# An RWKV recurrence and a SwiGLU layer on one core: single-token w, x transposed by DMA, and a new order of the steps

## The chip, the cores and the metric

The kernel runs on one core of one Trainium2 chip. A core has five engines that take their instructions in order, each from its own queue: TensorE (PE, matrix products, with its weight loads shown as PEld), VectorE (DVE), ScalarE (ACT), GpSimd (POOL) and SyncE (SP), which here only starts DMAs. They wait for one another by semaphores. The metric is the device time of one execution in microseconds (us). Three executions of the kernel before took 205.27, 206.77 and 207.02 us; their median is 206.77 us.

## The reference

Four batches, eight heads, 768 tokens, head dimension 48. Each head carries a 48 x 48 state through the tokens; the output of all heads of a token is a row of 384 numbers, which goes through RMS normalisation and a SwiGLU layer with 1536 hidden units.

```python
for t in range(S):
    cur = einsum('bhd,bhe->bhde', u * k[t], v[t])
    y[t] = einsum('bhd,bhde->bhe', r[t], state + cur)
    state = w[t][..., None] * state + einsum('bhd,bhe->bhde', k[t], v[t])
x = y, heads side by side          # 3072 tokens x 384
xn = x / sqrt(mean(x * x) + 1e-6) * rms_g
out = (silu(xn @ w_gate) * (xn @ w_val)) @ w_out
```

## The kernel before

The 768 tokens are cut into six superblocks of 128. A step such as `q_mm.2.1` is the function `q_mm` for superblock n = 2 and batch j = 1; one (n, j) is called a chunk. The kernel has no loops over chunks: a long string `ORDER` (lines 25 to 128) lists every step, and the kernel calls them one after another, so each engine's queue has its instructions in the order of that string. The PSUM banks are given out by rings (`psum`, line 223) to steps as they come, and tile pools give out SBUF buffers; a step that takes a buffer waits until its last reader is done.

**Recurrence of one chunk.** `load_w`, `load_r`, `load_k`, `load_v` (lines 252 to 271) start DMAs on SyncE's queue. `ln` (383) takes the logarithm of w on ScalarE. `cs_mm` (391) sums the logarithms over tokens with TensorE, `exp_r` and `exp_k` (426, 433) take exponentials on ScalarE, and `r_mul`, `k_mul` (444, 449) multiply r and k by them, with `k_mul` on VectorE or GpSimd by the table `K_POOL`. r and k are then transposed: for superblocks 0 and 1 by TensorE (`rk_pe`, 470), with a copy out of PSUM by `rk_tr` (476), for the others by a DMA transpose in `rk_tr`. `q_mm` (485) multiplies r with k for all pairs of tokens, `q_mask_e`, `q_copy_o` and `q_mask_o` (498 to 511) cut it to earlier tokens, `st_mm` and `st_new` (513, 523) carry the state, `y_mm` (532) forms y, and `bonus_mul`, `bonus_sum`, `bonus_v` (455 to 468, mostly GpSimd) form the term with u, which `x_add` (543) adds.

**w in pairs of tokens.** For superblocks 0 and 1 (`WIN = (0, 1)`, line 181) one load of 384 KB per batch brings w of both, with two consecutive tokens in a partition, one `ln` serves both, and `cs_mm` needs two matmuls for each sum and a second sum for k. For superblocks 2 to 5 each chunk has its own load of 192 KB and its own `ln`; `cs_mm` makes one sum, and `cs_add` (420) gets the sum for k from it on VectorE:

```python
if n in WIN:
    t = inp["w", 0, j] = pin.tile([128, 2 * DM], FP32, name="wt", bufs=NIN // 2)
    o = t.rearrange("p (h x) -> p h x", h=H)
    src = w[j, :, 0:2 * L, :].rearrange("h (p i) d -> p h (i d)", i=2)
```

**Normalisation.** `x_sq`, `x_rstd` and `xn_mul` (548 to 563) scale a chunk's x. For superblocks 0 to 3, `xn_pe` (574) transposes it on TensorE into PSUM, three matmuls, and `xn_out` (580) takes it out on VectorE, multiplied by rms_g. For superblocks 4 and 5, `xn_tr` (571) transposes it by a DMA on SyncE's queue, and `xn_gain` (591) multiplies it by rms_g in place, on GpSimd. Which of the two a chunk takes is only a matter of the steps that stand in `ORDER`.

**The layer.** Four chunks (512 tokens) make a group; there are six. For each group, `gate_mm` and `val_mm` (605, 609; the matmuls are at line 602) make twelve products each of three matmuls, `silu` (613) runs on ScalarE, `h_mul` (617) on VectorE; then `o_mm` (630) makes four output products of twelve matmuls, `o_out` copies them out and `out_dma` stores them. Groups 0 and 1 are made of batches 0, 1 and of batches 2, 3 of superblocks 0 and 1 (`COL`, line 193), so that group 0 can start before batches 2 and 3 have been loaded. While the products of one group run, the recurrence of the next superblock is worked between them. The weights come by `load_gv` and `load_wo` (348, 356) on GpSimd's DMA queue. ScalarE has two function tables, one for logarithm and exponential and one for silu, and `act` (232) loads a table whenever the other is in place. Steps called `warm` are matmuls of zeros that compute nothing.

The lines of the engines' steps are those of the profile, except that activations show the line of `act` (236).

## Time and profile before

| | |
|---|---|
| median of three executions | 206.77 us |
| the profiled execution | 206.26 us |
| its span, first to last instruction | 204.5 us |
| TensorE busy | 191.3 us, 94% |
| VectorE busy | 151.7 us, 74% |
| ScalarE busy | 144.4 us, 71% |
| GpSimd busy | 126.6 us, 62% |
| first gate matmul | 30.89 us after the start of the span |
| last group's first gate matmul | 178.00 us |

Times inside the span are counted from its start. The profile covers one execution. A busy TensorE need not be at its peak, since matmuls are pipelined and a matmul's duration is longer than the distance to the next one; what a step costs TensorE is read from start to start. A row of the timeline has start, length, engine, line, operation, output and inputs, shapes and count, and in square brackets how long the engine was idle before it and what ended that. A row of groups has the count, the busy time, the mean length of one in ns, and the idle time before. "DMA to landing" counts from issue until the data is there.

### The profile page before, as it was taken

What the parts mean: (1) busy time and instruction counts of PE and PEld (TensorE: products, weight loads), DVE (VectorE), ACT (ScalarE), POOL (GpSimd) and SP (SyncE); (2) the same over time, 40 slices, a digit from 0 to 9 for tenths busy, and PEclk for the clock granted to TensorE, in tenths of its full rate; (3) what the DMA queues carried; (4) which work ended last, traced back from release to release, by engine and by line L of the source; (5) the groups of instructions that cost most, each with busy time, mean ns of one, the idle gap of its engine ahead of it and who ended that gap; (6) DMA issues with size and microseconds to landing.
All of it is one profiled execution on the core that took longest, in us unless ns stands there. A gap on an engine that the chain in (4) does not pass through costs nothing.

```text
span 204.5 us, 4369 instructions
## 1 busy us (share of the span) xinstructions
PE 191.3 (94%) x1553; PEld 113.5 (55%) x1573; DVE 151.7 (74%) x298; ACT 144.4 (71%) x287; POOL 126.6 (62%) x186
## 2 busy tenths in 40 slices
PE   1995989999999999999999989999999999899996
PEld 1563654566665565664565644655655556455564
DVE  5169886599897999988999799978886782045720
ACT  4278797699998599977667697997885664046401
POOL 6569696279669954898892693769997736300000
PEclk9998599999999999999999999999999999999999
DMA  6999999999997999999979997985396310201212
GB/s 148 239 222 229 196 179 205 191 194 194 188 187 170 185 186 197 214 192 212 208 160 219 227 208 160 213 189 114 69 196 125 90 23 20 77 0 74 83 58 98
DMA packets 121566, 32.41 MB, mean 158 GB/s; under 512 B 116420, under 2 KB 120392, under 8 KB 121544
## 3 DMA queue, kind: packets, MB, share of 16 engines
q1 hardware_dynamic: 119504, 28.58, 66.8%
q0 software_dynamic: 2032, 3.54, 9.8%
q8 instruction: 12, 0.20, 0.4%
q14 instruction: 10, 0.08, 0.1%
q10 hardware_dynamic: 8, 0.00, 0.0%
HBM read 25.96 MB, written 4.72 MB: 150 GB/s over the span
## 4 chain that ended last, share of the span: by engine, by line
PE 69%; DMA 12%; POOL 8%; DVE 3%; issue 3%; ACT 2%; POOLq 1%; SPq 0%; DVEq 0%; ACTq 0%
PE ps_bu L602 10%; PE ps_av L602 9%; PE ps_au L602 9%; PE ps_bv L602 9%; PE ps_qz L634 5%; DMA wv_sb<-in_moe_w_val_dram 5%; PE ps_qx L634 4%; PE ps_qu L634 3%; DMA wo_sb<-in_moe_w_out_dram 3%; PE ps_qv L634 3%; DMA vt<-in_v_dram 2%; POOL ruk L458 2%; DMA rkT<-rk 1%; POOL ruk L457 1%; DMA xnt<-xn 1%
## 5 line engine op out<-in xcount | busy, mean ns | idle before, releaser
L620 DVE TENSOR_TENSOR ht<-ps_bu,sg 128x512 bf16<-128x512 f32 x38 | 26.1, 686 | 16.9 <-PE ps_bu L602 12.8
L634 PEld LDWEIGHTS <-ht 128*128 128x128 bf16 x300 | 28.3, 98 | 17.2 <-issue 0.4
L602 PEld LDWEIGHTS <-wg_sb 128*128 128x128 bf16 x216 | 23.7, 114 | 22.7 <-issue 2.3
L236 ACT ACTIVATE sg<-ps_av 128x512 bf16<-128x512 f32 x38 | 22.7, 597 | 14.0 <-PE ps_av L602 11.9
L602 PEld LDWEIGHTS <-wv_sb 128*128 128x128 bf16 x216 | 22.4, 115 | 17.9 <-DMA wv_sb<-in_moe_w_val_dram 0.4
L602 PE MATMUL ps_av<-xnt,wg_sb 128*128 128x512 bf16 x111 | 30.5, 379 | 0.4 <-DVE xnt L588 0.2
L602 PE MATMUL ps_bu<-xnt,wv_sb 128*128 128x512 bf16 x103 | 30.2, 381 | 0.6
L457 POOL TENSOR_TENSOR ruk<-rt,kt 128x384 f32<-128x384 f32 x24 | 24.7, 1028 | 9.2 <-DMA rt<-in_r_dram 8.7
L620 DVE TENSOR_TENSOR ht<-ps_bv,sg 128x512 bf16<-128x512 f32 x34 | 23.3, 686 | 8.5 <-PE ps_bv L602 5.2
L602 PE MATMUL ps_au<-xnt,wg_sb 128*128 128x512 bf16 x97 | 27.0, 380 | 1.2 <-POOL xnt L593 0.8
L236 ACT ACTIVATE sg<-ps_au 128x512 bf16<-128x512 f32 x34 | 20.3, 597 | 10.4 <-PE ps_au L602 8.3
L602 PE MATMUL ps_bv<-xnt,wv_sb 128*128 128x512 bf16 x101 | 27.6, 381 | 0.0
L458 POOL TENSOR_TENSOR ruk<-ruk,u_bc 128x384 f32<-128x384 f32 x24 | 24.6, 1024 | 1.9
L467 POOL TENSOR_TENSOR ydiag<-vt,diag 128x384 f32<-128x384 f32 x24 | 19.8, 831 | 5.7 <-DVE diag L462 5.7
L234 ACT ACT_TABLE_LOAD x16 | 20.5, 1283 | 1.9 <-PEq L673 1.6
L510 POOL TENSOR_SCALAR_AFFINE_SELECT qts<-qts 128x512 bf16<-128x512 bf16 x20 | 12.6, 638 | 13.3 <-ACT qts L503 13.3
L634 PE MATMUL ps_qz<-wo_sb,ht 128*128 128x384 bf16 x96 | 17.1, 326 | 0.2 <-DMA wo_sb<-in_moe_w_out_dram 0.2
L563 ACT ACTIVATE xn<-xb,rstd 128x384 bf16<-128x384 f32 x24 | 14.3, 606 | 3.8 <-POOL rstd L559 3.6
L550 ACT ACTIVATE junk<-xb 128x384 bf16<-128x384 f32 x24 | 12.4, 518 | 6.0 <-DVE xb L545 5.5
L634 PE MATMUL ps_qx<-wo_sb,ht 128*128 128x384 bf16 (+1 forms) x84 | 13.8, 315 | 0.0
L462 DVE TENSOR_REDUCE diag<-ruk 128x8 f32<-128x384 f32 x24 | 12.8, 542 | 0.5 <-POOL ruk L458 0.5
L236 ACT ACTIVATE lw<-wt 128x384 bf16<-128x384 f32 (+1 forms) x20 | 11.4, 579 | 1.5 <-DMA wt<-in_w_dram 1.4
(155 smaller groups left out, 370.4 us busy)
## 6 DMA issues: line engine op xcount, KB each, us to landing
kt<-in_k_dram SPq DMA_DIRECT2D x24, 192.0 KB, 4.2
rt<-in_r_dram SPq DMA_DIRECT2D x24, 192.0 KB, 3.9
vt<-in_v_dram SPq DMA_DIRECT2D x24, 192.0 KB, 3.8
out_dram<-ob SPq DMA_DIRECT2D x23, 192.0 KB, 3.0
wt<-in_w_dram SPq DMA_DIRECT2D x16, 192.0 KB, 4.1
wt<-in_w_dram SPq DMA_DIRECT2D x4, 384.0 KB, 4.2
wo_sb<-in_moe_w_out_dram POOLq DMA_DIRECT2D x3, 384.0 KB, 6.8
wg_sb<-in_moe_w_gate_dram POOLq DMA_DIRECT2D x1, 768.0 KB, 10.4
```

Source lines behind the costliest of these rows:

```text
L234: nc.scalar.preload_act_table_set(table_name)
L236: return nc.scalar.activation(**kw).ins
L457: nc.gpsimd.tensor_tensor(out=ruk[n, j], in0=inp["r", n, j], in1=inp["k", n, j], op=ALU.mult)
L458: nc.gpsimd.tensor_tensor(out=ruk[n, j], in0=ruk[n, j], in1=u_bc, op=ALU.mult)
L462: nc.vector.tensor_reduce(out=diag[n, j].rearrange("p h o -> p (h o)"), in_=ruk[n, j], axis=mybir.AxisListType.X, op=ALU.add)
L467: nc.gpsimd.tensor_tensor(out=ydiag[n, j], in0=inp["v", n, j], in1=diag[n, j].to_broadcast([128, H, D]), op=ALU.mult)
L510: nc.gpsimd.affine_select(out=qts[n, j][:, 1], in_=qts[n, j][:, 1], compare_op=ALU.is_gt, fill=0.0, base=0, pattern=[[0, NP], [1, 128]], c ...
L550: nc.scalar.activation(out=junk, in_=xb[n, j], func=AF.Square, accum_out=rstd[n, j][:, 0:1])
L563: nc.scalar.activation(out=xn, in_=xb[n, j], func=AF.Copy, scale=rstd[n, j][:, 1:2])
L602: nc.tensor.matmul(ps, lhsT=units(ws, c, f), rhs=xnt[n].rearrange("p (c x) -> p c x", c=KC)[:, c, :], start=(c == 0), stop=(c == KC - 1))
L620: nc.vector.tensor_tensor(out=ht[n][:, f, :], in0=bank.pop(("v", n, f)), in1=bank.pop(("sg", n, f)), op=ALU.mult)
L634: nc.tensor.matmul(ps[:, cols], lhsT=ht[n][:, f, b * L:(b + 1) * L], rhs=wo_sb[:, f, cols], start=(f == 0), stop=(f == FC - 1))
```

## The change

1. **w of batches 2 and 3 by single tokens.** `WIN` and `ONE_SUM` become sets of chunks. Superblocks 0 and 1 of batches 2 and 3 are loaded, logged and summed like those of the later superblocks: four loads of 192 KB in place of two of 384 KB, four `ln` of 384 columns in place of two of 768, one sum instead of two in each of the four `cs_mm`, and four more `cs_add`.
2. **x of superblocks 2 and 3 transposed by DMA.** Eight `xn_pe` and eight `xn_out` give way to eight `xn_tr` and eight `xn_gain`. `xn_gain` runs on VectorE for the chunks in `GAIN_DVE` (eight chunks of superblocks 2 to 5) and on GpSimd for the other eight.
3. **Other engines for single steps.** Four copies of transposed r and k go from ScalarE to VectorE (`RK_DVE`), three k products from VectorE to GpSimd (`K_POOL`), casts of v from seven on ScalarE to nine, the normalisation's square root from six on ScalarE to three, and output copies from thirteen on VectorE to eleven.
4. **A new order of all steps.** The first matmuls with u and rms_g become steps (`u_mm`, `u_out`, `g_mm`, `g_out`) that stand in the order too. More input loads stand ahead of the first gate matmul (37 instead of 24 loads), the `warm` steps that stood at the end of the order stand further ahead, and the function tables change 14 times instead of 16. Unused options are taken out, and `HALF`, which is empty, is put in.

```diff
-    CAST_ACT = sel("00 10 20 21 40 41 42")
+    CAST_ACT = sel("03 10 11 12 40 42 43 52 53")
-    K_POOL = sel("02 03 20 21 23 31 33 41 51 52 53")
+    K_POOL = sel("02 12 13 20 21 30 31 33 41 42 43 50 52 53")
-    WIN = (0, 1)
+    WIN = sel("00 01 10 11")
-    ONE_SUM = (2, 3, 4, 5)
+    ONE_SUM = sel("02 03 12 13 20 21 22 23 30 31 32 33 40 41 42 43 50 51 52 53")
-    GAIN_POOL = (4, 5)
+    GAIN_DVE = sel("21 22 23 33 41 42 50 51")
-    RK_DVE = sel("")
+    RK_DVE = sel("01 02 03 12")
-    RSTD_ACT = sel("00 01 02 11 32 42")
-    OUT_DVE = sel("00 01 02 10 11 13 21 22 33 40 43 50 53")
+    RSTD_ACT = sel("00 01 10")
+    OUT_DVE = sel("10 12 13 23 30 32 42 50 51 52 53")
+    HALF = ()
...
-        if n in WIN:
+        if (n, j) in WIN:
...
-        if n not in ONE_SUM:
+        if (n, j) not in ONE_SUM:
...
-    u_ps = psum("q", None, [128, DM])
-    nc.tensor.matmul(u_ps, lhsT=ones_row, rhs=u_row, start=True, stop=True)
-    nc.vector.tensor_copy(out=u_bc.rearrange("p h d -> p (h d)"), in_=u_ps)
...
+    def u_mm(n, j):
+        ps = bank["u", n, j] = psum("q", ("u", n, j), [128, DM])
+        nc.tensor.matmul(ps, lhsT=ones_row, rhs=u_row, start=True, stop=True)
+
+    def u_out(n, j):
+        nc.vector.tensor_copy(out=u_bc.rearrange("p h d -> p (h d)"), in_=bank.pop(("u", n, j)))
...
     def xn_gain(n, c):
         x = x_cols(*CHUNK.get((n, c), (n, c)))
-        nc.gpsimd.tensor_tensor(out=x, in0=x, in1=gT.to_broadcast([128, KC, L]), op=ALU.mult)
+        eng = nc.vector if (n, c) in GAIN_DVE else nc.gpsimd
+        eng.tensor_tensor(out=x, in0=x, in1=gT.to_broadcast([128, KC, L]), op=ALU.mult)
```

From the new order, the places of which the prediction speaks: the start, the boundary of superblocks 2 and 3, and the end of superblock 5 (steps left out are marked by dots):

```diff
+load_w.0.0 warm.20.0 warm.15.0 load_r.0.1 warm.17.0 load_w.0.1 load_r.0.0 load_k.0.0 load_k.0.1 load_k.1.0 u_mm.0.0
+ln.0.0 load_v.0.0 load_r.1.0 cs_mm.0.0 exp_r.0.0 load_v.1.1 load_v.1.0 load_v.0.1 load_r.1.1 load_k.1.1 load_w.0.2
...
+q_copy_o.2.2 q_mask_o.2.2 st_mm.2.3 y_mm.2.3 val_mm.1.2 st_mm.2.2 cs_mm.3.1 y_mm.2.2 x_add.2.3 h_mul.1.2 bonus_v.2.2
+x_add.2.2 x_sq.2.0 x_sq.2.3 x_rstd.2.0 x_rstd.2.3 cs_add.3.1 exp_r.3.1 bonus_sum.3.1 o_mm.1.2 o_out.1.2 exp_k.3.1
+xn_mul.2.3 xn_tr.2.3 x_sq.2.2 cs_add.3.0 st_new.2.3 load_v.3.3 k_mul.3.1 exp_r.3.0 xn_mul.2.0 xn_tr.2.0 x_rstd.2.2
+xn_mul.2.2 o_mm.1.3 o_mm.1.1 ln.3.2 r_mul.3.1 w_tot.3.1 w_tot.3.0 cast_v.3.0 xn_gain.2.1 r_mul.3.0 ln.3.3 exp_k.3.0
+ln.4.1 k_mul.3.0 xn_tr.2.2 xn_gain.2.0 load_r.4.2 load_k.3.3 cs_mm.3.2 cs_mm.3.3 out_dma.0.0 out_dma.1.2 rk_tr.3.0
+bonus_mul.3.2 bonus_mul.3.0 bonus_mul.3.3 xn_gain.2.3 cs_add.3.3 rk_tr.3.1 exp_k.3.3 k_mul.3.3 cs_add.3.2 o_mm.1.0
+xn_gain.2.2 val_mm.2.4 exp_r.3.3 r_mul.3.3 w_tot.3.3 exp_k.3.2 exp_r.3.2 w_tot.3.2 r_mul.3.2 load_v.3.1 cast_v.3.1
...
+val_mm.4.9 gate_mm.4.11 xn_mul.5.0 x_sq.5.1 h_mul.4.10 q_mask_e.5.2 q_mask_o.5.2 x_rstd.5.1 y_mm.5.2 val_mm.4.11
+h_mul.4.9 x_add.5.3 x_sq.5.3 silu.4.11 out_dma.3.3 xn_tr.5.0 val_mm.4.6 x_rstd.5.3 x_add.5.2 x_sq.5.2 x_rstd.5.2
+h_mul.4.6 h_mul.4.11 o_mm.4.2 xn_gain.5.0 xn_mul.5.3 o_mm.4.0 o_mm.4.3 o_mm.4.1 xn_mul.5.1 xn_mul.5.2 xn_tr.5.1
+xn_tr.5.2 xn_tr.5.3 o_out.4.0 out_dma.4.0 o_out.4.3 out_dma.4.3 xn_gain.5.2 xn_gain.5.3 xn_gain.5.1 gate_mm.5.0
```

More of the change, by code (lines that the diff above doesn't have):

```diff
@@ L211, in banks_of @@
             "val_mm": ("v",), "h_mul": ("v",), "o_mm": ("o",), "o_out": ("o",), "warm": ("warm",),
+            "u_mm": ("u",), "u_out": ("u",), "g_mm": ("gain",), "g_out": ("gain",),
         }
@@ L598, in units, with half_of_group @@
         return ws[g][:, c, a:a + FG * 128].rearrange("p (m i) -> p i m", i=FG)[:, f % FG, :]
+    def half_of_group(f):
+        h, p = f // (FC // 2), f % (FC // 2)
+        return slice(h * TS // 2, (h + 1) * TS // 2), 2 * p
     def fc_mm(ps, ws, n, f):
-        for c in range(KC):
-            nc.tensor.matmul(ps, lhsT=units(ws, c, f), rhs=xnt[n].rearrange("p (c x) -> p c x", c=KC)[:, c, :],
-                             start=(c == 0), stop=(c == KC - 1))
+        x = xnt[n].rearrange("p (c x) -> p c x", c=KC)
+        if n not in HALF:
+            for c in range(KC):
+                nc.tensor.matmul(ps, lhsT=units(ws, c, f), rhs=x[:, c, :], start=(c == 0), stop=(c == KC - 1))
+            return
+        cols, f = half_of_group(f)
+        for i in range(2):
+            for c in range(KC):
+                nc.tensor.matmul(ps[:, i * TS // 2:(i + 1) * TS // 2], lhsT=units(ws, c, f + i), rhs=x[:, c, cols],
+                                 start=(i == 0 and c == 0), stop=(i == 1 and c == KC - 1))
     def gate_mm(n, f):
```

241 lines of the change are left out of this document (112 added, 129 removed).

## The prediction

> **What bounds the kernel now.** I read the page's head and its chain of waits first, then the busy time of each engine by stretches cut where superblock groups change.
>
> ```profile
> span 204.5 us, 4369 instructions
> PE 191.3 (94%) x1553; PEld 113.5 (55%) x1573; DVE 151.7 (74%) x298; ACT 144.4 (71%) x287; POOL 126.6 (62%) x186
> ...
> PE 69%; DMA 12%; POOL 8%; DVE 3%; issue 3%; ACT 2%; POOLq 1%; SPq 0%; DVEq 0%; ACTq 0%
> ...
> 0.00:30.90 30.90, 22.97 (x232) 14.89 (x233) 20.64 (x49) 20.45 (x42) 22.79 (x39) 0.89 1.03 202
> 30.90:63.20 32.30, 31.88 (x284) 19.19 (x288) 26.61 (x55) 28.17 (x54) 21.25 (x32) 1.00 1.01 193
> 63.20:122.00 58.80, 57.47 (x493) 34.14 (x497) 53.64 (x107) 47.45 (x97) 44.40 (x62) 1.00 0.99 201
> 122.00:178.00 56.00, 54.39 (x418) 31.13 (x423) 40.80 (x74) 39.26 (x80) 38.17 (x56) 1.00 0.55 117
> 178.00:204.50 26.50, 24.61 (x136) 14.13 (x137) 10.02 (x16) 9.09 (x17) 0.00 (x0) 1.00 0.17 60
> ```
>
> The columns of the stretches are length, then PE, weight loads, DVE, ACT, POOL, the granted clock, the DMA share and GB/s. From 30.9 us on, TensorE is busy 168.35 of 173.6 us at clock 1.00: time in this part changes by TensorE work removed, or by waits closed or opened. Only about 5 us are idle there, so a new order has little left to win. Before 30.9 us TensorE is not the bound; a chain over VectorE and ScalarE is, beside a saturated DMA (share 1.03). VectorE is full in 63 to 122 (53.64 of 58.8), so what the change gives it there has thin cover.
>
> **TensorE work.**
>
> ```profile
> 41.38 0.49 PE L396 MATMUL ps_av<-lw,mw 128*128 128x384 bf16 x2
> ...
> 42.23 0.33 PE L520 MATMUL ps_qu<-vb,rk 128*128 128x96 bf16 x4
> ...
> 86.63 0.33 PE L578 MATMUL ps_qv<-ident,xn 128*128 128x128 bf16 x3
> 86.80 0.33 PE L411 MATMUL ps_au<-lw,mask_lt 128*128 128x384 bf16 x1
> ...
> 87.06 0.33 PE L578 MATMUL ps_qx<-ident,xn 128*128 128x128 bf16 x3
> ```
>
> From start to start, one chunk's transposes take 0.17 us (86.63 to 86.80). Eight chunks (superblocks 2, 3) leave TensorE: 1.36 us. A two-token cumulative sum takes 0.85 (41.38 to 42.23), a single-token one 0.26 (86.80 to 87.06). Four change, two of them behind the first gate matmul: 2 x 0.59 = 1.18; the other two lie in the start, where TensorE waits anyway, and count nothing. The new order moves three dummy matmuls in among the real ones behind the first gate; cold ones take 0.32 each (below), at twice the clock half of that: +0.48. Net on the path **-2.06 us**.
>
> **The start.**
>
> ```profile
> 5.95 0.50 PE L374 MATMUL ps_qx<-zero 128*128 128x384 bf16 x1
> ...
> 7.52 0.85 PE L396 MATMUL ps_au<-lw,mw 128*128 128x384 bf16 x2
> ...
> 14.65 0.23 PE L492 MATMUL ps_qv<-rkT 48*128 48x128 bf16 x1
> ...
> 30.89 0.81 PE L602 MATMUL ps_av<-xnt,wg_sb 128*128 128x512 bf16 x2 [0.20 <-DVE xnt L588]
> ...
> 16.41 0.68 DVE L507 TENSOR_TENSOR qts<-ps_qx,mask_lt 128x512 bf16<-128x512 f32 x1
> 17.00 0.54 DVE L451 TENSOR_TENSOR rk<-kt,ps_bv 128x384 bf16<-128x384 f32 x1
> ...
> 20.23 0.54 DVE L462 TENSOR_REDUCE diag<-ruk 128x8 f32<-128x384 f32 x1
> 20.69 0.54 DVE L527 TENSOR_TENSOR st<-ps_qx,wcol 128x384 bf16<-128x384 f32 x1
> ```
>
> Today the five dummies ahead of the first cumulative sum cost 7.52 - 5.95 = 1.57 us; in the new order none stands there, but the k tile of the first chunk is loaded fifth instead of second, so I take the first q matmul about 1.1 earlier, 13.55. From there to the first gate, 16.24 us today (14.65 to 30.89), VectorE has 29 instructions, 13.3 us at 0.59 for a mask and 0.47 for a 384-column one; in the new order 36, 17.4 us: one copy of transposed r and k moves to it from ScalarE (1.0, by ScalarE's row below), two additions for the single-token sums and two products with k come in, and work that now lies ahead of that q. VectorE then sets the start: 13.55 + 17.4 plus hops of 0.3 is 31.25, **+0.4**. Bounds -0.5 (other engines wait less) and +2.0 (the first q no earlier, and VectorE waits inside). All r, k, v and w of the first four chunks are among the first 14 loads; the additional ones fill SyncE's queue beside the weights, with the DMA saturated as now.
>
> **x by DMA: superblock 2.**
>
> ```profile
> 84.48 0.36 PE L540 MATMUL ps_qx<-vb,qts 128*128 128x48 bf16 x8
> ...
> 89.61 0.33 PE L578 MATMUL ps_qv<-ident,xn 128*128 128x128 bf16 x3
> ...
> L572 SPq DMA_TRANSPOSE xnt<-xn x8: 1182/1197/2382, 138.0 to 174.7; - x8
> ...
> DMA to landing us min/median/max: 2.3/2.5/3.5
> ...
> L588 DVE TENSOR_TENSOR xnt<-ps_qv,gT 128x384 bf16<-128x384 bf16 x6 | 3.3, 551 | 1.0 <-PE ps_qv L578 1.0
> L593 POOL TENSOR_TENSOR xnt<-xnt,gT 128x384 bf16<-128x384 bf16 x8 | 6.6, 830 | 8.2 <-DMA xnt<-xn 8.2
> L451 DVE TENSOR_TENSOR rk<-kt,ek 128x384 bf16<-128x384 f32 x11 | 8.0, 729 | 1.2 <-DMA kt<-in_k_dram 0.7 <-ACT ek L236 0.4
> ...
> 91.17 0.94 DVE L451 TENSOR_TENSOR rk<-kt,ek 128x384 bf16<-128x384 f32 x1
> ```
>
> Today the last y of superblock 2 ends at 84.7 and its last x is being transposed at 89.6, 4.9 us later. In the new order x then queues on SyncE behind another transpose (1.2 to issue, with a load between), lands 2.5 after its issue and is multiplied by rms_g on VectorE. No row has this form: bounds 0.55 (its PSUM form) and 0.94 (the longest two-SBUF-input product quoted); I take 0.55, the same shape. 4.9 + 1.2 + 2.5 + 0.55 = 9.15. The cover is four output products and two sums of 0.26; an output product takes 1.95 (next fence): 8.3 in all. TensorE then waits about 0.9, against almost nothing now: **+0.9**, from 0 to +2.2 (landing 3.5, gain 0.94, less the cover). While x waits at the head of SyncE's queue, the load of superblock 3's last k and two output stores wait behind it, and for that k the bonus product at the head of GpSimd's queue; superblock 3's q is five us behind the first gate, so it costs nothing while that delay is below 5.
>
> The Trainium skill (SBUF — State Buffer, "Who interferes with whom") says that a VectorE instruction with two SBUF inputs shares a read interface with GpSimd's SBUF reads and one blocks the other; this speaks against moving the gain from PSUM to SBUF operands. The rows agree (729 ns mean for two SBUF inputs, 551 from PSUM), and by the rule this term is 0.2 to 0.4 larger.
>
> ```profile
> 118.70 0.32 PE L411 MATMUL ps_av<-lw,mask_lt 128*128 128x384 bf16 x1 [0.66 <-ACT ek L236]
> ```
>
> For **superblock 3** the same chain of 9.15 runs beside four output products and four sums, 8.8, so it opens some 0.4. Today's order has a stall of its own in that place, a cumulative sum that waits 0.66 us for an exponential, and in the new order these sums stand where their PSUM banks are long free. Together I take 0; bounds -0.7 (the stall goes and x is in time) and +1.7 (landing 3.5, gain 0.94).
>
> **The last superblock.**
>
> ```profile
> 142.34 1.95 PE ps_qx L634 x12
> ...
> 182.05 0.65 PE ps_bv L602 x3
> ...
> 169.00 0.36 PE L540 MATMUL ps_qx<-vb,qts 128*128 128x48 bf16 x8
> ...
> 178.00 0.81 PE L602 MATMUL ps_au<-xnt,wg_sb 128*128 128x512 bf16 x2 [0.83 <-POOL xnt L593]
> ...
> 177.12 0.83 POOL L593 TENSOR_TENSOR xnt<-xnt,gT 128x384 bf16<-128x384 bf16 x1 [0.44 <-DMA xnt<-xn]
> ```
>
> The last y ends at 169.2, the gate starts at 178.0: 8.8 us, covered by 4 x 1.95 = 7.8; TensorE idles 0.83. The new order adds two products of 0.65 behind the last y: 9.1 of cover. Its last x is third on SyncE rather than last of two (+1.2), less the two gains that go to VectorE: I take a stall of 0.3, **-0.5** (-0.8 to +0.7).
>
> **Elsewhere.** VectorE gets four copies, four sums and eight gains, and loses eight PSUM outputs, three k products and two output copies; GpSimd gets three k products and three square-root chains for two casts; ScalarE is relieved and has two table loads fewer. A copy of 1024 columns out of PSUM is not in the trace on VectorE; the bounds are 0.55, the form with 384 columns, and 1.01, ScalarE's copy of this shape:
>
> ```profile
> L483 ACT COPY rkT<-ps_qu 128x1024 bf16<-128x1024 bf16 x2 | 2.0, 1012 | 0.0
> ```
>
> I take 1.0. VectorE has 4 x 1.0 + 4 x 0.5 more and 3 x 0.73 + 2 x 0.5 less, about 3 us; GpSimd seven instructions more at its mean of 0.68 (126.6 / 186), some 5 us, spread over all superblocks. I cost both at nothing behind the start: TensorE's queue hides them, since from 30.9 to 63.2 VectorE has 5.7 us of room and GpSimd 11, and from 63.2 to 122 5.2 and 14. Where that room goes, the excess is paid in full: up to +3 if all of VectorE's falls on a full stretch. Of ScalarE's relief I take nothing either, as it is nowhere the fullest but in 30.9 to 63.2 (28.17 of 32.3), where VectorE now takes over its copies.
>
> On SyncE's queue eight more transposes cost 8 x 1.2 = 9.6 us of issuing, in two groups of four. Behind them stand loads for the superblock after the next; their lead, a whole group of gate and value products, hides 4.8 us per group. If it didn't, r and k at GpSimd would be late next.
>
> ```profile
> wt<-in_w_dram SPq DMA_DIRECT2D x16, 192.0 KB, 4.1
> wt<-in_w_dram SPq DMA_DIRECT2D x4, 384.0 KB, 4.2
> ```
>
> The w of batches 2 and 3 comes in four loads of 192 KB instead of two of 384: equal bytes, latency 4.1 against 4.2, all needed later than what is queued ahead. Nothing, up to +0.8 while DMA is saturated.
>
> **Sum.** The profiled execution took 206.26 us (204.5 span, 1.76 around it). -2.06 + 0.4 + 0.9 + 0 - 0.5 = -1.26: **205.0 us**. The median of the runs before is 206.77, 0.25% above the profiled one; I leave that.
>
> **Rivals.**
> *The order closes waits.* About 5 us of idle remain behind the first gate, and two table loads fewer and earlier loads bear on it; if half of it goes, 205.0 - 2.5 = 202.5. Against it: those waits are short and many. By 1.8 or more 0.23.
> *The saved matmul time is only waiting time.* VectorE's 17.4 us of start and its room of 5.2 go: the -2.06 is given back, about 207. 0.11.
> *x arrives late* (slower). Place: the gates of superblocks 2 and 3. If transposes land after 3.5 under a DMA share of 0.99 instead of 2.5, and the gains stand behind a bonus product on GpSimd, each boundary waits 3 us in place of 0.9 and 0: +5.1. A wait also costs clock:
>
> ```profile
> 15.00:20.00 5.00, 2.72 (x39) 1.96 (x38) 4.67 (x10) 4.36 (x8) 4.87 (x6) 0.90 1.05 234
> 20.00:25.00 5.00, 4.74 (x56) 3.04 (x54) 4.10 (x10) 4.01 (x10) 3.15 (x6) 0.50 1.14 194
> ```
>
> After 2.3 idle us in 15 to 20, TensorE ran at 0.50. About 2 us at half clock is 1 us lost; 205.0 + 5.1 + 1 = 211. It decides from where the chain is 1.7 us longer than its cover at both boundaries, +2.5 together. 0.28. The Trainium skill (TensorE: Matmul & The Clock Gate, "What's actually happening") halves the clock after an idle window of about 3.4 us; by that rule the stalls of my forecast cost no clock and this rival's may.
>
> **How the numbers follow.** Forecast 0.38, the three rivals 0.23, 0.11, 0.28. A measurement here tells about 1% from no change, that is 204.7 and 208.8. The forecast (203 to 207) lies half on each side of 204.7: 0.19 and 0.19. Faster 0.19 + 0.23 = 0.42; same 0.19 + 0.09 = 0.28; slower 0.02 + 0.28 = 0.30. Downward the bounds of the four terms leave 205.0 - 0.9 - 0.9 - 0.7 - 0.3 = 202.2, and closing about a third of the 5 idle us besides 200.5; upward they come to 205.0 + 1.6 + 1.3 + 1.7 + 1.2 + 0.8 = 211.6, and the late x to 211. The range 200.5 to 211 leaves out about a tenth on each side.
>
> **What would show it.** Right: first gate at 31 to 32; TensorE busy some 2 us less behind it; waits of the gates of superblock 2 for x of about 1 us, of the last below 0.5. Wrong: a first gate beyond 33, idle of 3 us or a clock below 1.00 behind it, VectorE or GpSimd full across a boundary, or waits for r and k at GpSimd that grow.

## The result, and the profile after

The changed kernel takes 218.52 us (218.26 to 220.83) against 206.02 us (205.05 to 207.02) of the kernel before: ratio 1.066, 95% interval 1.061 to 1.071. It is 12.5 us slower, outside the predicted range. A ratio here counts only executions that agree with the fastest of their kernel; where those of an experiment fall apart, the single times are given.

The head of the page of the changed kernel and its chain of waits:

```profile
span 216.6 us, 4302 instructions
...
PE 193.9 (90%) x1521; PEld 111.8 (52%) x1521; DVE 155.8 (72%) x301; ACT 139.5 (64%) x281; POOL 131.9 (61%) x193
...
PE 55%; DMA 15%; SPq 11%; ACT 9%; issue 3%; DVE 3%; POOL 2%; POOLq 0%; ACTq 0%; DVEq 0%
```

TensorE had 69% of the chain, now 55%; SyncE's queue, which had nothing of it, has 11%, and ScalarE 9% instead of 2%. To find the places I cut both traces where the first product of a group starts. Columns: length, then PE, weight loads, DVE, ACT, POOL, granted clock, DMA share, GB/s. The first three of six stages, of the kernel before, then of the changed one:

```profile
30.89:63.22 32.33, 31.91 (x284) 19.22 (x288) 26.64 (x55) 28.20 (x54) 21.29 (x32) 1.00 1.01 193
63.22:91.73 28.51, 28.35 (x246) 16.95 (x247) 26.39 (x54) 24.74 (x49) 22.03 (x32) 1.00 0.98 190
91.73:122.05 30.32, 29.15 (x249) 17.22 (x252) 27.29 (x54) 22.75 (x49) 22.40 (x30) 1.00 1.00 210
```

```profile
31.30:68.05 36.75, 33.34 (x281) 19.98 (x281) 28.33 (x57) 28.05 (x55) 23.99 (x35) 0.95 0.93 179
68.05:100.06 32.01, 28.14 (x238) 16.47 (x236) 25.89 (x50) 25.52 (x48) 23.85 (x35) 0.98 0.84 171
100.06:131.81 31.75, 30.81 (x236) 16.79 (x237) 26.06 (x51) 22.32 (x47) 23.41 (x34) 0.91 0.87 182
```

The span grew by 12.1 us: 0.4 ahead of the first gate, then 4.4, 3.5 and 1.4 in these stages, and 1.9, -0.1 and 0.5 in the last three (30.27, 27.54, 26.98 against 28.34, 27.61, 26.50). Over all six, idle time of TensorE (length less PE) rose from 5.2 to 14.6 us, that is 9.4. Its busy time rose by 2.3 though its work fell: the granted clock is below 1.00 in three stages. If the work is 2.06 us less, as forecast, matmuls at half clock added an estimated 4.4 us to it. The growth of the span is the sum of 0.4 at the start, 9.4 of idle and 2.3 of busy time: 12.1. The 0.5 us of the last stage lie behind TensorE's last product, which ends 23.5 us after the gate in both kernels.

Two places stand out. The first is behind the first gate. Rows of the changed kernel's timeline for ScalarE, and the product that waits:

```profile
33.51 0.52 ACT L239 ACTIVATE lw<-wt 128x384 bf16<-128x384 f32 x1 [3.27 <-DMA wt<-in_w_dram]
...
34.05 1.28 ACT L237 ACT_TABLE_LOAD   x1
35.34 0.60 ACT L239 ACTIVATE sg<-ps_av 128x512 bf16<-128x512 f32 x1
...
36.72 1.00 PE L605 MATMUL ps_bu<-xnt,wv_sb 128*128 128x512 bf16 x3 [2.66 <-DVE ht L634]
```

The gate's first product ends at 32.1, but its silu starts at 35.34: `ln.1.2`, the logarithm of w of superblock 1, batch 2, stands ahead of it on ScalarE and waits 3.27 us for its load. The profile names VectorE as TensorE's releaser; VectorE waits for that silu.

The second is the boundary of superblock 2:

```profile
88.12 1.28 ACT L237 ACT_TABLE_LOAD   x1
...
90.68 0.52 ACT L546 ACTIVATE junk<-xb 128x384 bf16<-128x384 f32 x1
...
91.60 1.32 ACT L559 ACTIVATE xn<-xb,rstd 128x384 bf16<-128x384 f32 x2
...
92.72 4.68 SPq L568 DMA_TRANSPOSE xnt<-xn  x2
...
98.50 0.99 POOL L453 TENSOR_TENSOR ruk<-rt,kt 128x384 f32<-128x384 f32 x1
98.53 1.38 DVE L590 TENSOR_TENSOR xnt<-xnt,gT 128x384 bf16<-128x384 bf16 x1 [1.98 <-DMA xnt<-xn]
...
100.06 1.44 PE L605 MATMUL ps_bv<-xnt,wv_sb 128*128 128x512 bf16 x3 [3.86 <-DVE xnt L590]
...
101.30 1.49 PE L605 MATMUL ps_av<-xnt,wg_sb 128*128 128x512 bf16 x3
```

The last x is ready at 92.9, its transposition has landed at 98.5, the product with rms_g takes 1.38 instead of 0.55, and TensorE stands 3.86 us. The next products then follow one another by 1.24 to 1.28 us instead of 0.65. Two stretches of 5 us show the granted clock, which is the third number from the end (0.86, then 0.50):

```profile
95.00:100.00 5.00, 1.20 (x8) 0.49 (x5) 3.02 (x5) 2.95 (x5) 2.40 (x4) 0.86 0.39 78
100.00:105.00 5.00, 4.94 (x12) 1.76 (x13) 3.30 (x7) 1.50 (x3) 4.84 (x6) 0.50 1.05 234
```

### The profile page after: what moved, and what is told of

Its sections match the earlier page's. It is cut to its first block, busy times and chain, and to the rows that moved or that the text cites. A ratio compares the mean times of both kernels' runs of the same rounds, so it can differ in the third digit from the quotient of the medians.

```text
span 216.6 us, 4302 instructions
## 1 busy us (share of the span) xinstructions
PE 193.9 (90%) x1521; PEld 111.8 (52%) x1521; DVE 155.8 (72%) x301; ACT 139.5 (64%) x281; POOL 131.9 (61%) x193
## 4 chain that ended last, share of the span: by engine, by line
PE 55%; DMA 15%; SPq 11%; ACT 9%; issue 3%; DVE 3%; POOL 2%; POOLq 0%; ACTq 0%; DVEq 0%
PE ps_av L605 11%; PE ps_bu L605 9%; PE ps_au L605 9%; PE ps_bv L605 9%; SPq L247 8%; DMA xnt<-xn 6%; DMA wt<-in_w_dram 6%; PE ps_qx L648 5%; ACT L237 3%; PE ps_qz L648 2%; PE ps_qv L648 2%; SPq L259 2%; ACT junk L546 2%; DMA kt<-in_k_dram 2%; DMA rkT<-rk 1%
## 5 line engine op out<-in xcount | busy, mean ns | idle before, releaser
L605 PEld LDWEIGHTS <-wv_sb 128*128 128x128 bf16 x216 | 23.3, 115 | 28.2 <-issue 9.2
L634 DVE TENSOR_TENSOR ht<-ps_bu,sg 128x512 bf16<-128x512 f32 x36 | 24.7, 686 | 16.5 <-PE ps_bu L605 10.6
L605 PE MATMUL ps_bv<-xnt,wv_sb 128*128 128x512 bf16 x108 | 29.9, 386 | 5.4 <-DVE xnt L590 3.9
L239 ACT ACTIVATE sg<-ps_au 128x512 bf16<-128x512 f32 x35 | 20.9, 597 | 20.5 <-PE ps_au L605 18.4
L605 PE MATMUL ps_av<-xnt,wg_sb 128*128 128x512 bf16 x111 | 31.6, 395 | 0.6 <-DVE xnt L584 0.6
L634 DVE TENSOR_TENSOR ht<-ps_bv,sg 128x512 bf16<-128x512 f32 x36 | 24.7, 686 | 10.3 <-PE ps_bv L605 8.2
L605 PE MATMUL ps_au<-xnt,wg_sb 128*128 128x512 bf16 x105 | 29.1, 387 | 1.8 <-POOL xnt L590 1.8
L454 POOL TENSOR_TENSOR ruk<-ruk,u_bc 128x384 f32<-128x384 f32 x24 | 25.5, 1062 | 1.9
L447 POOL TENSOR_TENSOR rk<-kt,ek 128x384 bf16<-128x384 f32 x14 | 14.1, 1022 | 3.5 <-ACT ek L239 3.0
L546 ACT ACTIVATE junk<-xb 128x384 bf16<-128x384 f32 x24 | 12.5, 519 | 3.7 <-DVE xb L541 3.4
L648 PE MATMUL ps_qu<-wo_sb,ht 128*128 128x384 bf16 (+1 forms) x84 | 13.9, 314 | 0.0
```

The source lines that it names most:

```text
L239: return nc.scalar.activation(**kw).ins
L447: eng.tensor_tensor(out=rk[:, n % 2, j, 1, :, 0:D], in0=inp["k", n, j], in1=bank["cs_k", n, j][:, 0:DM].rearrange("p (h d) -> p h d", h=H) ...
L454: nc.gpsimd.tensor_tensor(out=ruk[n, j], in0=ruk[n, j], in1=u_bc, op=ALU.mult)
L546: nc.scalar.activation(out=junk, in_=xb[n, j], func=AF.Square, accum_out=rstd[n, j][:, 0:1])
L605: nc.tensor.matmul(ps, lhsT=units(ws, c, f), rhs=x[:, c, :], start=(c == 0), stop=(c == KC - 1))
L634: nc.vector.tensor_tensor(out=ht[n][:, f, :], in0=v, in1=sg, op=ALU.mult)
```

## Experiments: the logarithm ahead of the silu

Each experiment has a short name, given in brackets. Names with an a are edits of the changed kernel, names with a b of the kernel before. Diffs of the order show only the steps that move. A ratio is against the kernel before, run beside it; its median went from 204.20 to 207.04 us from one experiment to another, so medians of different experiments can be compared to about 1 us only.

**One step moved (a_ln12).** Theory: in-order waiting on ScalarE. Rival: w of batches 2, 3 is late for all of its readers.

```diff
-val_mm.0.1 ln.1.2 silu.0.1
+val_mm.0.1 silu.0.1
-silu.0.8 h_mul.0.8
+silu.0.8 ln.1.2 h_mul.0.8
```

> The changed kernel with one step moved: the logarithm of w of superblock 1, batch 2 stands behind the sixth silu of the first group instead of ahead of the first. Theory (ScalarE's queue): that logarithm waits 3.27 us for a load that is far behind in a saturated DMA, holds the first silu back, TensorE idles 2.66 us and then runs at half clock; the stage from the first gate to the second group is 4.45 us longer than before. Moved, the stage loses 4 us or more: about 214.3 us. Rival (DMA): w of batches 2, 3 is late for everybody, and the cumulative sum of that chunk waits instead; then at most 1.5 us go, 217.

Measured: 212.38 us, ratio 1.031 (1.025 to 1.037); 6.1 us less than the changed kernel, or 7.2 by the two ratios. Its first stage:

```profile
31.51:64.76 33.25, 31.80 (x281) 19.34 (x281) 28.24 (x57) 26.95 (x55) 24.07 (x35) 1.00 1.03 200
```

It takes 33.25 instead of 36.75 us, at full clock and with no wait for a silu: 3.5 us are shown to hang on the place of the logarithm. The second stage takes 30.19 instead of 32.01, as the wait for x shrank to 2.04 us: the last two transposes of x took SyncE 2.92 us to issue instead of 4.68. Whether that, and the rest of the gain in later stages, follows from the moved logarithm is not settled. The load itself is no earlier: it landed 14.8 us after its issue, at 36.6, ahead of the logarithm's new place at 43.76.

**Part 1 undone (a_pairs).** w of batches 2, 3 by pairs again.

```diff
-    WIN = sel("00 01 10 11")
+    WIN = sel("00 01 02 03 10 11 12 13")
-load_w.1.2 load_w.1.3 ln.1.2 ln.1.3 cs_add.0.2 cs_add.0.3 cs_add.1.2 cs_add.1.3
```

> The changed kernel with part 1 undone: w of batches 2, 3 of superblocks 0, 1 by pairs again, at the places of the loads and logarithms of superblock 0; the steps of superblock 1 for them and four additions go. Theory (place): the wait ahead of the first silu goes as with the moved logarithm (212.4 us), TensorE gets 1.18 us of sums back: 213 to 214 us. Rival (the split itself costs DMA time): 211 us or less.

Measured: 213.36 us, ratio 1.038 (1.032 to 1.045). The wait ahead of the first silu is gone here too, and the time is not below that of a_ln12, as it would be if the split itself were the cost. The total agrees with the theory, but not by its sum: the first gate is 2.0 us later than in a_ln12 (33.52 against 31.51), which is not explained, and TensorE's busy time in the first stage rose by 0.4 us (32.22 against 31.80) instead of 1.18.

**The load moved instead (a_early; a_early_fix2, with x of superblock 2 as in a_fix2 of the next section).** Is it the place of the logarithm, or that of its load?

```diff
-load_w.1.3 load_k.0.2 load_k.0.3 bonus_mul.0.0 k_mul.0.0 cast_v.0.0 load_w.1.2
+load_w.1.3 load_w.1.2 load_k.0.2 load_k.0.3 bonus_mul.0.0 k_mul.0.0 cast_v.0.0
```

> The changed kernel with only one load moved: w of chunk 1.2 two loads earlier on SyncE's queue, ahead of k of chunks 0.2 and 0.3; the logarithm stays ahead of the first silu. Theory (this load is issued at 21.46 us, when GpSimd's weights are already in the DMA, and lands 12.0 us later; 1.4 us earlier it lies ahead of most of them): it lands before 30 us, the wait of 3.27 us on ScalarE goes, about 212.5 us as with the moved logarithm. Rival (anything issued from 19 us on lands late): the wait stays or goes over to the k behind it, 216 us or more.

> The load moved as in a_early and x of superblock 2 transposed by TensorE as in a_fix2, no logarithm moved. Theory (these two are the main losses, and the moved logarithm itself cost 0.92 us): 208 us, 1% above the kernel before. Rival (as in a_early): 212 us or more.

Measured: a_early took 222.39, 218.79, 221.19 and 224.25 us in its four executions, a_early_fix2 218.55 us, ratio 1.063 (1.058 to 1.068). The rival came true: the logarithm no longer waits, but the k that is now behind it does. For the second kernel, VectorE's row and the times of its k loads from issue to landing:

```profile
37.88 0.56 DVE L447 TENSOR_TENSOR rk<-kt,ek 128x384 bf16<-128x384 f32 x1 [9.85 <-DMA kt<-in_k_dram]
```

```profile
DMA to landing us min/median/max: 3.5/4.1/15.9
```

The first gate starts at 41.04 us. So no single load is badly placed: whichever load SyncE issues just behind the start of the weights is late. When the weights start, the first and the last of four loads in the kernel before, and the first two and the last in the changed one (GpSimd's queue):

```profile
18.69 0.99 POOL L351 DMA_DIRECT2D wg_sb<-in_moe_w_gate_dram  x1
...
29.57 0.85 POOL L351 DMA_DIRECT2D wv_sb<-in_moe_w_val_dram  x1
```

```profile
20.74 0.99 POOL L339 DMA_DIRECT2D wv_sb<-in_moe_w_val_dram  x1
21.73 0.78 POOL L339 DMA_DIRECT2D wg_sb<-in_moe_w_gate_dram  x1
...
24.91 0.80 POOL L339 DMA_DIRECT2D wv_sb<-in_moe_w_val_dram  x1
```

The old order starts the 2.3 MB within 10.9 us, the new one within 4.2. In the old order the last w that is needed before the first products was issued at 16.26, ahead of all weights; in the new one w of chunk 1.2 at 21.46, behind the first. The old order has late loads of its own. Its loads of r, issued from 10 to 50 us:

```profile
DMA to landing us min/median/max: 4.0/8.7/14.6
```

The slowest was issued at 25.75 and landed at 40.4; a k of that time took 12.1 us. But from 25 to 50 us no instruction of VectorE, ScalarE or GpSimd waits for an input load there, and no w took more than 4.6. So late loads beside the weights are not new; that the first silu stands behind one is.

**The weights spread out (a_gv; a_gv_fix2, with x of superblock 2 as in a_fix2).**

```diff
-load_gv.1.0 bonus_v.1.1
+bonus_v.1.1
-load_gv.1.1 y_mm.1.1
+load_gv.1.0 y_mm.1.1
-bonus_mul.0.3 bonus_mul.0.2
+load_gv.1.1 bonus_mul.0.3 bonus_mul.0.2
```

> The changed kernel with only two of the four weight loads on GpSimd's queue moved back: the 768 KB of the gate by two steps of GpSimd to about 25 us, the 768 KB of the value product to about 29.5 us. Loads, logarithm, x by DMA as in the changed kernel. Theory (the 2.3 MB of weights, started within 4.2 us, hold up the loads on SyncE's queue): w of chunk 1.2 lands by 28 us, the waits ahead of the first silu go, 212.5 us. Rival (the DMA is full anyway, with 24 loads ahead of the weights): the same load still lands after 31 us, 216 us or more.

> The same with x of superblock 2 transposed by TensorE as in a_fix2; no logarithm and no input load moved. Theory (two causes, late loads behind the weights and x of superblock 2 by DMA): 208 us. Rival: as in a_gv, 212 us or more.

Measured: a_gv took 219.82, 218.53, 214.42 and 212.00 us in its four executions, a_gv_fix2 209.17 to 213.34, ratio 1.030 (1.024 to 1.036). Two executions of a_gv are near the theory's time and two above the rival's 216. The edit moved the third start of weights only from 23.31 to 24.03 us, and the fourth from 24.91 to 29.48. a_gv and a_gv_fix2 differ in no queue before the x of superblock 2, yet their profiles differ. ScalarE and SyncE in a_gv, then in a_gv_fix2:

```profile
37.60 0.52 ACT L239 ACTIVATE lw<-wt 128x384 bf16<-128x384 f32 x1 [7.44 <-DMA wt<-in_w_dram]
```

```profile
21.61 1.04 SPq L259 DMA_DIRECT2D wt<-in_w_dram  x1
```

```profile
29.96 0.51 ACT L239 ACTIVATE lw<-wt 128x384 bf16<-128x384 f32 x1
```

```profile
21.14 0.70 SPq L259 DMA_DIRECT2D wt<-in_w_dram  x1
```

Issued at 21.14, the load lands 7.4 us later and is there when the logarithm comes at 29.96; issued at 21.61 it lands at 37.6, 16.0 us after its issue. It looks like a race between SyncE's last loads and the weights, run anew in each execution. Twelve profiles have this same load behind the first start of the weights, by 0.1 to 1.1 us: it landed 7.4 to 16.8 us after its issue. The longest times are those furthest behind (16.0 and 16.8 us at 0.95 and 1.09), but 0.12 us behind it was 10.8 and 0.73 behind it was 9.6, so the moment of issue does not decide it alone. That the weights hold the load up is argued from this order in time; no run leaves them out. The race can also explain why some of these kernels scatter: one with the changed kernel's start (a_pe2, below) was profiled with a k that VectorE awaited for 4.37 us and a first gate at 35.99. The kernels whose products do not depend on such a load (a_ln12 and those built on it) took 208.0 to 215.1 us, with one execution of a_ln12_warm at 217.36.

## Experiments: x by DMA

**Part 2 in the old order (b_tr).** The eight `xn_out` go, too.

```diff
-xn_pe.2.0 xn_pe.2.1 xn_pe.2.2 xn_pe.2.3 xn_pe.3.0 xn_pe.3.1 xn_pe.3.2 xn_pe.3.3
+xn_tr.2.0 xn_tr.2.1 xn_tr.2.2 xn_tr.2.3 xn_tr.3.0 xn_tr.3.1 xn_tr.3.2 xn_tr.3.3
-val_mm.2.10
+xn_gain.2.1 xn_gain.2.0 xn_gain.2.2 xn_gain.2.3 val_mm.2.10
-val_mm.3.2
+xn_gain.3.0 xn_gain.3.2 xn_gain.3.3 xn_gain.3.1 val_mm.3.2
```

> The kernel before, in its own order, with x of superblocks 2 and 3 transposed by DMA at the places of TensorE's transposes, the four multiplications by rms_g just ahead of the next group's first product (21, 22, 23, 33 on VectorE, the others on GpSimd). Theory (the way by DMA is itself too long for the cover of four output products): TensorE saves 1.36 us and waits 2 to 4 us at both boundaries, with loss of clock: 209 to 213 us. Rival (only the new order's places are bad): waits below 1 us each, 205 to 207.

Measured: 219.16 us, ratio 1.058 (1.050 to 1.067), more than either expected. TensorE's first product of the two groups, and ScalarE:

```profile
97.87 1.44 PE L601 MATMUL ps_bu<-xnt,wv_sb 128*128 128x512 bf16 x3 [7.29 <-DVE xnt L592]
...
132.78 1.10 PE L601 MATMUL ps_bu<-xnt,wv_sb 128*128 128x512 bf16 x3 [4.16 <-POOL xnt L592]
```

```profile
89.80 0.61 ACT L562 ACTIVATE xn<-xb,rstd 128x384 bf16<-128x384 f32 x1 [2.00 <-DMA xnt<-xn]
```

7.29 and 4.16 us of waiting, and half clock behind both. The last row is a cost that I had not seen: `xn` has three buffers, each is held until its transposition by DMA has landed, and the scaling of the fourth x waits 2.00 us for that.

**x of superblock 2 back on TensorE, in the new order (a_pe2; a_ln12_pe2, with the logarithm moved).** The first form put the transposes near the places of the products with rms_g. The steps that went and came, without their places:

```diff
-xn_tr.2.1 xn_gain.2.1 xn_tr.2.0 xn_tr.2.3 xn_tr.2.2 xn_gain.2.0 xn_gain.2.3 xn_gain.2.2
+xn_pe.2.1 xn_out.2.1 xn_pe.2.0 xn_out.2.0 xn_pe.2.3 xn_out.2.3 o_out.1.3 xn_pe.2.2 xn_out.2.2
```

> The changed kernel with x of superblock 2 transposed by TensorE again (x of superblock 3 still by DMA), the transposes standing where the multiplications by rms_g stood; one output copy (chunk 1.3) stands a little earlier to free a PSUM bank. Theory (transposes by DMA): the 3.86 us of idle ahead of the second-to-third group boundary and the 2.7 us lost to half clock behind it go, 4 x 0.17 us of TensorE come: about 212.6 us. Rival (ScalarE): the last x itself is late because its square and its scaling stand behind a table load and exponentials on ScalarE; then a wait of 1.5 us or more remains with its clock, and at most 3 us go, 215.5 or more.

> Both edits together. If both theories hold and the two losses are separate, the gains add: about 208.4 us, 2 to 3 us above the kernel before, the rest being spread over the later boundaries. If one only uncovers the other, the sum falls short by 2 us or more: 210.5 and above.

Measured: 217.47, 211.08, 217.33 and 216.56 us without the moved logarithm (the race above), and 212.57 us with it, ratio 1.030 (1.023 to 1.036): no gain on a_ln12. In that profile the wait for x is gone, but an output product and the gate wait 0.65 us each for `xnt`, and another output product 0.77 us: with one PSUM bank to spare, each transposition has to be taken out before the next step can go on. That profile also has its first group at half clock at first (34.85 us against 33.25 in a_ln12), so its total is not a measure of this boundary alone. The form with banks freed (a_fix2), as the main steps that moved:

```diff
-st_new.2.3
+st_new.2.3 st_new.2.2
-xn_gain.2.1 xn_tr.2.2 xn_gain.2.0 cs_mm.3.2 cs_mm.3.3
+xn_pe.2.3 xn_pe.2.0 cs_mm.3.2 cs_mm.3.3
-xn_gain.2.3 cs_add.3.3 exp_k.3.3
+xn_out.2.3 xn_out.2.0 cs_add.3.3 o_out.1.3 exp_k.3.3
-o_mm.1.0 xn_gain.2.2
+xn_pe.2.2 o_mm.1.0 xn_out.2.2
```

> The changed kernel with the logarithm moved (212.4 us) and x of superblock 2 transposed by TensorE, this time with PSUM banks freed for it: the state of chunk 2.2 and the output copy of chunk 1.3 are taken out earlier, and no transposition waits for a copy. Theory (the way of x by DMA makes the 2.04 us of idle at this boundary and the half clock behind it, 1.7 us): 212.4 - 3.7 + 0.7 = 209.4 us. Rival (something else is equally late there, as when the squares were moved): 211.5 us or more.

Measured: 209.16 us, ratio 1.014 (1.007 to 1.021), where 209.4 was expected. The group starts without a wait and at full clock:

```profile
94.72 0.81 PE L605 MATMUL ps_bv<-xnt,wv_sb 128*128 128x512 bf16 x3
95.37 0.81 PE L605 MATMUL ps_av<-xnt,wg_sb 128*128 128x512 bf16 x3
```

So with x of superblock 2 off the DMA, and a state and an output copy taken out earlier to make room for it, 3.2 us go once the logarithm is out of the way (212.38 - 209.16; 3.6 by the two ratios). By stages, only 0.1 of it is in the stage that ends with the wait: there 2.04 us of waiting go, but TensorE is busy 0.96 us longer (29.10 against 28.14) and waits 0.77 us for an x. The stage behind it is 2.3 us shorter: 1.7 us of half clock are gone, and the wait at its end falls from 1.34 to 0.70. What x by DMA cost here is for the most part the clock behind the wait.

**Superblock 3 too (a_fix)**, in the same manner; the last part of the moved steps:

```diff
-xn_tr.3.2 xn_tr.3.1 xn_tr.3.3 cs_mm.4.3 xn_gain.3.2 xn_gain.3.1 o_mm.2.2 xn_gain.3.3
+xn_pe.3.1 cs_mm.4.3 xn_out.3.1 st_new.3.0 o_out.2.3 xn_pe.3.3 xn_out.3.3 xn_pe.3.2 o_mm.2.2 xn_out.3.2
```

> The same for superblocks 2 and 3, that is, the changed kernel with the logarithm moved and part 2 undone. Theory (the 1.34 us at the boundary of superblock 3 are x by DMA too, though the profile names the sum of w there): 209.4 - 1.34 + 0.7 = 208.8 us. Rival (VectorE or ScalarE is what ends last at that boundary): no better than with superblock 2 alone, 209.5 us or more.

Measured: 212.57 us, ratio 1.029 (1.023 to 1.036), 3.4 us worse than with superblock 2 alone. TensorE now waits among its output products:

```profile
117.20 2.11 PE L648 MATMUL ps_qv<-wo_sb,ht 128*128 128x384 bf16 x12 [0.65 <-DVE xnt L584]
...
124.26 0.33 PE L574 MATMUL ps_qx<-ident,xn 128*128 128x128 bf16 x3 [0.74 <-DVE st L523]
...
127.56 0.81 PE L605 MATMUL ps_bv<-xnt,wv_sb 128*128 128x512 bf16 x3 [0.73 <-ACT ek L239]
```

For superblock 3 this says nothing of the way by DMA; it says that my placing of the transposes was worse than a wait of 1 us.

**ScalarE's order (a_ln12_x).** Is it rather the table load and the exponentials ahead of the last square?

```diff
-x_sq.2.0 x_sq.2.3 x_rstd.2.0 x_rstd.2.3 cs_add.3.1 exp_r.3.1 bonus_sum.3.1 o_mm.1.2 o_out.1.2 exp_k.3.1
+x_sq.2.0 x_sq.2.3 x_sq.2.2 x_rstd.2.0 x_rstd.2.3 x_rstd.2.2 cs_add.3.1 bonus_sum.3.1 o_mm.1.2
-xn_mul.2.3 xn_tr.2.3 x_sq.2.2 cs_add.3.0 st_new.2.3
+xn_mul.2.3 xn_tr.2.3 xn_mul.2.0 xn_tr.2.0 xn_mul.2.2 xn_tr.2.2 exp_r.3.1 o_out.1.2 exp_k.3.1 cs_add.3.0 st_new.2.3
```

> The changed kernel with the logarithm moved as before (212.4 us) and, at the end of superblock 2, the squares, square roots and scalings of its last three x moved ahead of the exponentials of superblock 3 and of their table load on ScalarE, and the three transposes issued one behind the other. Theory (ScalarE's order delays the last x): the 2.04 us of idle and about 1.7 us of half clock at that boundary go, 208.5 to 209.5 us. Rival (issue and landing of the transposes set it): the wait stays above 1 us, 211 us or more.

Measured: 213.57 us, ratio 1.037 (1.030 to 1.043): no gain, but not for the rival's reason. The gate no longer waits; two sums wait for logarithms that are now late, and the wait at the next boundary is 2.01 instead of 1.34 us:

```profile
91.69 0.32 PE L406 MATMUL ps_au<-lw,mask_lt 128*128 128x384 bf16 x1 [0.97 <-ACT lw L238]
...
92.84 0.34 PE L406 MATMUL ps_av<-lw,mask_lt 128*128 128x384 bf16 x1 [0.74 <-ACT lw L238]
```

**The clock by itself (a_ln12_warm).** Twelve dummies, matmuls of zeros, fill the wait at the end of superblock 2.

```diff
-o_mm.1.0 xn_gain.2.2 val_mm.2.4
+o_mm.1.0 xn_gain.2.2 warm.30.0 warm.31.0 warm.32.0 warm.33.0 warm.34.0 warm.35.0 warm.36.0 warm.37.0 warm.38.0 warm.39.0 warm.40.0 warm.41.0 val_mm.2.4
-st_new.2.3
+st_new.2.3 st_new.2.2
```

> The changed kernel with the logarithm moved (212.4 us), x by DMA kept, and twelve matmuls of zeros (0.16 us each, 1.9 us together) ahead of the first product of the group behind superblock 2, so that TensorE does not stand idle there. Theory (half of what the wait costs is clock): the products behind it run at full clock, -1.5 us: 210.9 us. Rival (the clock does not follow the idle time there): 212.4 us or more, as the matmuls only fill the wait.

Measured: 213.31 us, ratio 1.033 (1.023 to 1.043).

```profile
93.70 4.50 PE L356 MATMUL ps_qx<-zero 128*128 128x384 bf16 x12
98.03 0.81 PE L605 MATMUL ps_bv<-xnt,wv_sb 128*128 128x512 bf16 x3
98.68 0.81 PE L605 MATMUL ps_av<-xnt,wg_sb 128*128 128x512 bf16 x3
```

The products behind do run at full clock, and that stage takes 29.16 instead of 31.18 us: the half clock cost 2.0. But the dummies, all into one bank, took 4.33 us instead of 1.9, so nothing is won. The total is in the rival's range, but not for its reason: the clock does follow the wait here, as the theory has it.

**All products with rms_g of superblocks 3 to 5 on VectorE (a_fix2_gd).**

```diff
-    GAIN_DVE = sel("21 22 23 33 41 42 50 51")
+    GAIN_DVE = sel("20 21 22 23 30 31 32 33 40 41 42 43 50 51 52 53")
```

> a_fix2 (209.2 us) with the multiplications by rms_g of superblocks 3 to 5 all on VectorE. Theory (at those boundaries the multiplication on GpSimd, 0.83 us and behind products with k and u, is what ends last, and its reads lengthen those of VectorE to 1.03 us): the waits of 0.70 and 0.91 us ahead of the groups of superblocks 3 and 4 shrink by 0.3 to 0.5 us each: 208.4 us. Rival (the landing of the transposes decides, and VectorE now waits for them in order, ahead of its other work): 209.2 us or more.

Measured: 213.58 us, ratio 1.047 (1.042 to 1.051); a_fix2 beside its own run of before had 1.014. The rival holds: VectorE waits for landings in order, and the products themselves lengthen.

```profile
120.31 2.32 DVE L590 TENSOR_TENSOR xnt<-xnt,gT 128x384 bf16<-128x384 bf16 x2
```

```profile
125.35 0.61 PE L605 MATMUL ps_bv<-xnt,wv_sb 128*128 128x512 bf16 x1 [2.44 <-DVE xnt L590]
```

```profile
157.78 0.84 PE L605 MATMUL ps_au<-xnt,wg_sb 128*128 128x512 bf16 x2 [3.11 <-DVE xnt L590]
```

## Experiments: parts 1 and 3 in the old order, and what remains

**Part 1 in the old order (b_w1).**

> The kernel before, in its own order, with part 1 alone: w of batches 2, 3 of superblocks 0, 1 by single tokens, each new load and logarithm right behind the one that it was split from, each new addition right behind its sum. Theory (the loss of the first group is one of place: a logarithm ahead of the silu whose load comes late): here no such place exists, TensorE saves up to 1.18 us behind the first gate: 205 to 206.5 us. Rival (the split itself costs, by more and smaller pieces in a saturated DMA): everything behind them lands later, 208.5 us or more.

```diff
-load_w.0.3 ln.0.3 cs_mm.0.3 cs_mm.1.3
+load_w.0.3 load_w.1.3 ln.0.3 ln.1.3 cs_mm.0.3 cs_add.0.3 cs_mm.1.3 cs_add.1.3
```

(The same for batch 2.) Measured: 208.99 us, ratio 1.016 (1.009 to 1.024). The rival is the nearer one: the first gate is at 32.65, and in the first group TensorE waits for an exponential and for a product behind it:

```profile
45.43 0.81 PE L602 MATMUL ps_bu<-xnt,wv_sb 128*128 128x512 bf16 x3 [1.07 <-ACT ek L236]
...
48.41 0.81 PE L602 MATMUL ps_av<-xnt,wg_sb 128*128 128x512 bf16 x3 [0.75 <-DVE wcol L441]
```

**Part 3 in the old order (b_eng).** This one takes CAST_ACT, K_POOL, RK_DVE, RSTD_ACT and OUT_DVE of the changed kernel, nothing else:

> The kernel before, in its own order, with part 3 alone: the copies of transposed r and k, the products with k, the casts, the square roots and the output copies on the engines of the changed kernel. Theory (other engines hide it behind TensorE's queue): 205.5 to 207.5 us. Rival (VectorE, full between 63 and 122 us, is pushed over by the copies): 209 us.

Measured: 216.15 us, ratio 1.048 (1.041 to 1.056), 10 us slower. The first group alone takes 36.71 us instead of 32.33, with a cast of v that now stands on ScalarE behind a table load and an exponential:

```profile
46.14 0.33 PE L519 MATMUL ps_qv<-vb,rk 128*128 128x96 bf16 x4 [1.86 <-ACT vb L378]
```

In an order made for other engines none of the three parts is free. They can't be added up (2.8 + 12.7 + 9.9 us is twice the whole loss), and they don't show what each costs in the order made for it.

**What remains (a_fix2_cs).** Last, on top of a_fix2, the sum that waits for the moved logarithm:

```diff
-cs_mm.1.2 cs_add.1.2 st_new.0.2
+st_new.0.2
-y_mm.0.3 bonus_v.0.2
+y_mm.0.3 cs_mm.1.2 cs_add.1.2 bonus_v.0.2
```

> a_fix2 (209.2 us), and the cumulative sum of chunk 1.2 with its addition moved behind the y of chunk 0.3, so that it no longer waits 0.92 us for the moved logarithm on TensorE. Theory (order, not data, makes the remaining waits of the first group): the 0.92 and 0.43 us of idle at 44 to 46 us go, 207.9 us. Rival (the exponentials of that chunk become late and a later product waits instead): 209 us or more.

Measured: 208.29 us against 204.20 us of the kernel before on that chip, ratio 1.021 (1.016 to 1.025): no better than a_fix2, since a later product waits 1.64 us there for an exponential. The 1.4 to 2% that are left with both causes gone are not settled. What the profile of a_fix2 shows are waits below 1 us: 0.92 at 44 us for the moved logarithm, 0.77 at 85, 0.70 and 0.91 ahead of the groups of superblocks 3 and 4 (x by DMA), 0.93 at 129 for a k product on GpSimd. No version tried beats the kernel before.

## Why the prediction was wrong

- **TensorE work, -2.06: right in total, in part by luck.** In a_ln12 TensorE is busy 167.9 us behind the first gate, 1.7 of them the extra of 3.4 us at half clock: 166.2, against 168.35 - 2.06 = 166.3. But 1.08 of the fall lies in the last stage (24.61 to 23.53), where six dummies at the end of the old order went, which the sum does not count; the five stages before it lost 1.1 us. By parts, the sums by single tokens saved 0.4 us (a_pairs) where 1.18 was counted, and x of superblock 2 saved 0.96 (a_fix2) where 0.68 was.
- **The start, +0.4: right, by luck** (31.30 against 30.89). The first q came at 12.62 instead of the forecast 13.55, and VectorE, busy 17.2 us from there to the gate (forecast 17.4), was idle for 1.5 us instead of 0.3: two errors of about 1 us cancel. a_pe2, with the same start, was profiled with 35.99.
- **The step that failed most** is the one on w: "all needed later than what is queued ahead. Nothing, up to +0.8 while DMA is saturated", with the sentence that the additional loads only "fill SyncE's queue beside the weights". I counted loads of the first four chunks and did not follow `ln.1.2`, which stands ahead of the first silu on ScalarE, to its load, the 22nd, behind the start of the weights. It waited 3.27 us there, and with the logarithm moved (a_ln12) the first stage is 3.5 us shorter and the whole 6.1. For SyncE and GpSimd the prediction named what is queued behind a waiting instruction; for ScalarE it did not.
- **Superblock 2, +0.9, bounds 0 to +2.2: the mechanism right, the size too small.** Waited were 3.86 us, and about 2.6 more went to the clock (four products at 1.27 us instead of 0.65, and part of the next), for which the sum has nothing. The 4.9 us to the last x were right (5.0: 87.9 to 92.9). Behind it I put 1.2 + 2.5 + 0.55 = 4.25; it took 7.0 (92.9 to 99.9): the transposition ahead of it on SyncE took 2.04 us to issue, its own landed 3.65 us after issue, and the product with rms_g took 1.38. Most of this had rows in the trace of before (issue up to 2.38, landing up to 3.5), and I took the medians. With the other loss gone, taking x off the DMA still gained 3.2 us (a_fix2), outside the bounds.
- **The Trainium skill's rule** (SBUF — State Buffer, "Who interferes with whom"), that a VectorE instruction with two SBUF inputs and GpSimd's SBUF reads block each other, agrees with one row here: 1.38 us beside a GpSimd product against 0.55. I had worked out 0.2 to 0.4 from means; it was 0.83.
- **Superblock 3, 0** (-0.7 to +1.7): a wait of 0.94 us, inside, which the profile puts down to a step on w (`wcol`) and not to x. **The last superblock, -0.5:** its wait is 1.01 instead of 0.83 us, so +0.2, inside the bounds but the other way. **Elsewhere, nothing:** the boundary of superblock 4 waits 0.79 us where it had none. I had not looked at it, as its x went by DMA before too.
- **The rivals.** "x arrives late" was the right one for one boundary of two, and its clock was priced at 1 us instead of 2.6. That I gave it no logarithm ahead of a silu is why even its 211 falls short. The Trainium skill's rule on the clock (TensorE: Matmul & The Clock Gate, "What's actually happening"), an idle window of about 3.4 us, was no safe bound: a wait of 2.04 us was followed by half clock in a_ln12, and one of 3.11 us in a_fix2_gd was not.
- **The range** was built from terms of one boundary at a time. It had no case in which a single wait for a load in the first group costs 3.5 us and more.

## What to carry to other kernels

Follow every instruction that may wait for a transfer to what stands behind it in the same in-order queue, on all engines, and compare the issue time of its load with the start of any bulk transfer, rather than with the order of the loads. A step moved from a busy engine to a DMA has to be priced with the slow issues and landings in the trace rather than their medians, with the buffers that it holds meanwhile, and with the clock that TensorE loses in the wait. Where a kernel's order and its assignment of steps to engines were made for each other, single parts of a change can't be priced in the other's order.
